# Linear attention on one core: stores deferred behind loads, a part of relu(k) on GpSimd, eps by 32-row matmuls, all queues reordered

## The chip, the cores and the metric

One NeuronCore of a Trainium2 chip. Times are device microseconds of one execution, median of several; the profile's span is about 2 us shorter than the time (177.9 of 179.64 us in the profiled run of the kernel before). Each ratio compares runs of the same rounds; the changed kernel was timed in rounds of its own. Changes under 2% count as "same" unless the interval says otherwise.

## The reference

```python
# q, k, v: bf16 [1, 32, 2048, 128]
def reference(q, k, v):
    phi_q = jnp.where(q > 0, q + 1, jnp.exp(q)) + 1e-6
    phi_k = jnp.where(k > 0, k + 1, jnp.exp(k)) + 1e-6
    kv = jnp.einsum("bhsd,bhse->bhde", phi_k, v)
    z = jnp.einsum("bhsd->bhd", phi_k)
    num = jnp.einsum("bhqd,bhde->bhqe", phi_q, kv)
    den = jnp.einsum("bhqd,bhd->bhq", phi_q, z)[..., None] + 1e-6
    return num / den
```

There are 32 heads. 50.3 MB are read and 16.8 MB written.

## The kernel before

Both phi are computed as min(exp(x), 1) + eps plus relu(x): the two summands stay apart and both go through TensorE. The kernel keeps its tiles in two on-chip memories: SBUF, which loads fill and stores empty, and PSUM, to which TensorE writes its products. v gets a column of ones, so kv also holds z. A head takes, by engine:

- ScalarE: exp(k), exp(q) of the transposed q in PSUM, half or all of relu(q), the copy of kv out of PSUM.
- VectorE: min and relu of k for two heads at a time, min(q), the other half of relu(q), reciprocals and the divide (numerator in PSUM times the reciprocal).
- TensorE: 16 transposes of q, 32 products for kv, 32 half-products (two for each of 16 row tiles, one per summand of phi) for the numerators. These lie in six PSUM banks of two or three tiles; one eps matmul per bank starts the bank and puts 1e-6 in its denominator columns. The numerators come in three groups of two banks (A, B, C).
- GpSimd: the copy of v beside the ones. SyncE: all loads, and all stores but the last part of the last head, in one queue.

The program is a set of named operations with dependencies; the order on each engine is a fixed list.

```python
    NI = 8                                   # input buffers, in heads
    NO = 6                                   # output buffers
    LAG = 2
    VLAG = 3; VAFTER = "rA"                  # the copy of v starts after a reciprocal of group A
    RELU_Q = "SSSA" * (NH // 4)              # S: half on ScalarE, half on VectorE; A: all on ScalarE
    ...
        for h in range(NH + LAG - 1):
            if h + NI < NH:
                loads(h + NI)
            if h >= LAG:
                store(h - LAG)
    ...
        def numerator(e, h, tiles):          # one bank
            s = h % 2
            e.matmul(_ap(o_ps[:, :], SLOT[tiles[0]] + D, [[NC, len(tiles)]]), lhsT=ones[:], rhs=epsr[:, 0:len(tiles)],
                     start=True, stop=False, skip_group_check=True)
            for t in tiles:
                o = o_ps[:, SLOT[t]:SLOT[t] + NC]
                e.matmul(o, lhsT=emq_sb[:, s, t * P:(t + 1) * P], rhs=kvs_sb[:, s, :], start=False, stop=False, ...)
                ins = e.matmul(o, lhsT=rq_sb[:, s, t * P:(t + 1) * P], rhs=kvs_sb[:, s, :], start=False, stop=True, ...)
            return ins
        def num(which, h, banks, deps, bank=None):
            def f(e):
                for b in banks:
                    ins = numerator(e, h, BANKS[b])
                return ins
    ...
        def relu_k(h, n):                    # n = 2 heads in one instruction on VectorE
            ...
            add("DVE", key, lambda e: e.tensor_scalar(
                rk_sb[:, s:s + n], k_sb[:, b:b + n], 0.0, None, op0=ALU.max), ...)
```

Of the kernel before, what the change touches and what calls it, by code (L numbers as in the profile page):

```python
# [7 lines left out]
EPS = 1e-6  # L8
# [7 lines left out]
class Program:  # L16
# [20 lines left out]
    def resolve(self):  # L37
# [5 lines left out]
        for bank, keys in self.banks.items():  # L43
            order = self.schedule[bank]
            assert sorted(order) == sorted(keys), (bank, set(order) ^ set(keys))
            for a, b in zip(order, order[1:]):
                if self.ops[a]["eng"] != self.ops[b]["eng"]:
                    self.ops[b]["deps"].append(a)
        value, count = {}, {}
# [48 lines left out]
def _eps_pieces():  # L98

    import struct  # L100

    def bf(x):
        u = struct.unpack("<I", struct.pack("<f", x))[0]
        u = (u + 0x7FFF + ((u >> 16) & 1)) & 0xFFFF0000
        return struct.unpack("<f", struct.pack("<I", u))[0]

    a = bf(EPS / 128)
    b = bf(EPS - 126 * a)
    return a, b, bf(EPS - 126 * a - b)


def bass_standalone__linear_attn_elu__prompt_kernel(nc: bass.Bass, q: bass.AP, k: bass.AP, v: bass.AP, out: bass.AP):
# [4 lines left out]
    bf16, fp32, i32 = mybir.dt.bfloat16, mybir.dt.float32, mybir.dt.int32  # L117
# [3 lines left out]
    NO = 6  # L121
    L = NH - 1

    LAG = 2
    VLAG = 3
    VAFTER = "rA"
    VFROM = 3
    VTO = 31
    LATE = {L - 1: dict(D="DVE", B="DVE", C="ACT"), L: dict(D="DVE", B="DVE", C="ACT")}
    V1_DVE = 1  # L130
    FUSED = [0] * NH
# [4 lines left out]
    WARM1 = 22  # L136
    FIRST = [("k", 0), ("q", 0), ("v", 0)]
    RELU_Q = "SSSA" * (NH // 4)
# [3 lines left out]
            "warm0 T0 warm1 T1 kx0 kv0 nC0 nA0 T2 nB0 kx1 kv1 nC1 kx2 kv2 nA1 T3 nC2 nB1 kx3 kv3 nB2 nA2 T4 nC3 kx4 kv4 nB3 "  # L142
            "nA3 T5 nC4 kx5 kv5 nB4 nA4 T6 nC5 kx6 kv6 nB5 nA5 T7 nC6 kx7 kv7 nB6 nA6 T8 nC7 kx8 kv8 nB7 nA7 T9 nC8 kx9 kv9 "
            "nB8 nA8 T10 nC9 kx10 kv10 nB9 nA9 T11 nC10 kx11 kv11 nB10 nA10 T12 nC11 kx12 kv12 nB11 nA11 T13 nC12 kx13 kv13 "
            "nB12 nA12 T14 nC13 kx14 kv14 nB13 nA13 T15 nC14 kx15 kv15 nB14 nA14 T16 nC15 kx16 kv16 nB15 nA15 T17 nC16 kx17 "
            "kv17 nB16 nA16 T18 nC17 kx18 kv18 nB17 nA17 T19 nC18 kx19 kv19 nB18 nA18 T20 nC19 kx20 kv20 nB19 nA19 T21 nC20 "
            "kx21 kv21 nB20 nA20 T22 nC21 kx22 kv22 nB21 nA21 T23 nC22 kx23 kv23 nB22 nA22 T24 nC23 kx24 kv24 nB23 nA23 T25 "
            "nC24 kx25 kv25 nB24 nA24 T26 nC25 kx26 kv26 nB25 nA25 T27 nC26 kx27 kv27 nB26 nA26 T28 nC27 kx28 kv28 nB27 nA27 "
            "T29 kx29 kv29 nB28 nA28 T30 nC28 kx30 kv30 nA29 nB29 nC29 T31 kx31 kv31 nD30 nC30 nB30 nD31 nC31 nB31 ").split(),
        DVE=(  # L150
            "eps0 ones v1ones0 v1ones1 eps1 eps2 rk0 em0 emq0 rqb0 rk1 v10 emq1 rqb1 rk2 rC0 fC0 em1 em2 rk3 rqb2 emq2 rA0 "
            "fA0 em3 rC1 fC1 rk5 rC2 fC2 em5 rA1 fA1 emq3 rA2 fA2 rk7 rC3 fC3 rqb4 emq4 rA3 fA3 em7 rC4 emq5 rqb5 fC4 rA4 fA4 "
            "rk9 rC5 rqb6 emq6 fC5 rA5 fA5 em9 rC6 fC6 emq7 rA6 fA6 rk11 rC7 rqb8 emq8 fC7 rA7 fA7 em11 rC8 rqb9 emq9 fC8 rA8 "
            "fA8 rk13 rC9 rqb10 emq10 fC9 rA9 fA9 em13 rC10 emq11 fC10 rA10 fA10 rk15 rC11 rqb12 emq12 fC11 rA11 fA11 em15 "
            "rC12 rqb13 emq13 fC12 rA12 fA12 rqb14 rC13 emq14 fC13 rk17 rA13 fA13 emq15 rC14 fC14 em17 rA14 fA14 rk19 rC15 "
            "rqb16 emq16 fC15 rA15 fA15 em19 rC16 rqb17 emq17 fC16 rA16 fA16 rqb18 rC17 emq18 fC17 rk21 rA17 fA17 emq19 rC18 "
            "fC18 em21 rA18 fA18 rk23 rC19 rqb20 emq20 fC19 rA19 fA19 em23 rC20 rqb21 emq21 fC20 rA20 fA20 rqb22 rC21 emq22 "
            "fC21 rk25 rA21 fA21 emq23 rC22 em25 fC22 rA22 fA22 rk27 rC23 rqb24 emq24 fC23 rA23 fA23 em27 rC24 rqb25 emq25 "
            "fC24 rA24 fA24 emq26 rC25 rqb26 rk29 fC25 rA25 fA25 emq27 rC26 em29 fC26 rA26 fA26 rk31 rC27 rqb28 emq28 rA27 "
            "fA27 em31 rqb29 fC27 rA28 fA28 emq29 rC28 fC28 rqb30 emq30 rC29 fC29 rA29 fA29 emq31.0 emq31.1 rD30 fD30 rC30 "  # L160
            "rB30 fB30 rD31 fD31 rC31 rB31 fB31 ").split(),
        ACT=(
            "ek0.0 ek0 eq0 rqa0 ek1 eq1 kvs0 rqa1 ek2 eq2 kvs1 rqa2 ek3 kvs2 ek4 ek5 eq3 rqa3 kvs3 ek6 eq4 rqa4 kvs4 ek7 eq5 "
            "rqa5 kvs5 ek8 eq6 rqa6 kvs6 ek9 eq7 rqa7 kvs7 ek10 eq8 rqa8 kvs8 ek11 eq9 rqa9 kvs9 ek12 eq10 rqa10 kvs10 ek13 "
            "eq11 rqa11 kvs11 ek14 eq12 rqa12 kvs12 ek15 eq13 rqa13 kvs13 ek16 eq14 rqa14 kvs14 ek17 eq15 rqa15 kvs15 ek18 "
            "eq16 rqa16 kvs16 ek19 eq17 rqa17 kvs17 ek20 eq18 rqa18 kvs18 ek21 eq19 rqa19 kvs19 ek22 eq20 rqa20 kvs20 ek23 "
            "eq21 rqa21 kvs21 ek24 eq22 rqa22 kvs22 ek25 eq23 rqa23 kvs23 ek26 eq24 rqa24 kvs24 ek27 eq25 rqa25 kvs25 ek28 "
            "eq26 rqa26 kvs26 ek29 eq27 rqa27 kvs27 ek30 eq28 rqa28 kvs28 ek31 eq29 rqa29 kvs29 eq30 rqa30 kvs30 eq31.0 "
            "eq31.1 rq31.0 rq31.1 kvs31 fC30.12 fC30.13 fC30.14 fC30 fC31.12 fC31.13 fC31.14 fC31 stC31 ").split(),
        POOL=(  # L170
            "ident0 ident v11 v12 v13 v14 v15 v16 v17 v18 v19 v110 v111 v112 v113 v114 v115 v116 v117 v118 v119 v120 v121 "
            "v122 v123 v124 v125 v126 v127 v128 v129 v130 v131 ").split(),
        kv=(
            "kx0 kv0 kvs0 nC0 rC0 fC0 kx1 kv1 kvs1 nC1 kx2 kv2 kvs2 rC1 fC1 nC2 rC2 fC2 kx3 kv3 kvs3 nC3 kx4 kv4 rC3 fC3 kvs4 "
            "nC4 kx5 kv5 rC4 kvs5 fC4 nC5 kx6 kv6 rC5 kvs6 fC5 nC6 kx7 kv7 rC6 fC6 kvs7 nC7 kx8 kv8 rC7 kvs8 fC7 nC8 kx9 kv9 "
            "rC8 kvs9 fC8 nC9 kx10 kv10 rC9 kvs10 fC9 nC10 kx11 kv11 rC10 kvs11 fC10 nC11 kx12 kv12 rC11 kvs12 fC11 nC12 kx13 "
            "kv13 rC12 kvs13 fC12 nC13 kx14 kv14 rC13 kvs14 fC13 nC14 kx15 kv15 rC14 fC14 kvs15 nC15 kx16 kv16 rC15 kvs16 "
            "fC15 nC16 kx17 kv17 rC16 kvs17 fC16 nC17 kx18 kv18 rC17 kvs18 fC17 nC18 kx19 kv19 rC18 fC18 kvs19 nC19 kx20 kv20 "
            "rC19 kvs20 fC19 nC20 kx21 kv21 rC20 kvs21 fC20 nC21 kx22 kv22 rC21 kvs22 fC21 nC22 kx23 kv23 rC22 kvs23 fC22 "
            "nC23 kx24 kv24 rC23 kvs24 fC23 nC24 kx25 kv25 rC24 kvs25 fC24 nC25 kx26 kv26 rC25 kvs26 fC25 nC26 kx27 kv27 rC26 "  # L180
            "kvs27 fC26 nC27 kx28 kv28 rC27 kvs28 kx29 kv29 kvs29 fC27 nC28 kx30 kv30 rC28 fC28 kvs30 nC29 rC29 fC29 kx31 "
            "kv31 nC30 kvs31 rC30 fC30.12 fC30.13 fC30.14 fC30 nC31 rC31 fC31.12 fC31.13 fC31.14 fC31 ").split())
# [4 lines left out]
    with ExitStack() as es:  # L187
# [38 lines left out]
        add("DVE", "eps0", lambda g: g.memset(epsr[:], ea))  # L226
        add("DVE", "eps1", lambda g: g.memset(epsr[0:1, :], eb), ["eps0"])
        add("DVE", "eps2", lambda g: g.memset(epsr[32:33, :], ec), ["eps0"])
        add("DVE", "ones", lambda g: g.memset(ones[:], 1.0))
        for s in range(2):  # L230
            add("DVE", f"v1ones{s}", lambda g, s=s: g.memset(v1_sb[:, s, :, D:NC + 1], 1.0))


        def load(name, dst, src, h, freed, parts=1):
            n = NT // parts
            for r in range(parts):
# [3 lines left out]
                    [f.format(h - NI) for f in freed if h >= NI] + (GATE if f"{name}{h}" == "k1" else []), dma=f"{name}{h % NI}" if parts == 1 else f"{name}{h}.{r}")  # L240

        def loads(h):
            load("k", k_sb, kf, h, ["ek{}", "rk{}"])
            load("q", q_sb, qf, h, ["T{}"])
            load("v", v_sb, vf, h, ["v1{}"])

        def ld(name, h):
            return [f"ld{name}{h}.0", f"ld{name}{h}.1"] if h == 0 and name == "k" else [f"ld{name}{h}"]
# [5 lines left out]
        for name, h in FIRST:  # L254
            load(name, dict(k=k_sb, q=q_sb, v=v_sb)[name], dict(k=kf, q=qf, v=vf)[name], h, [], 2 if h == 0 and name == "k" else 1)
        for h in range(max(h for _, h in FIRST) + 1, min(NI, NH)):
            loads(h)
        for h in range(NH + LAG - 1):
            if h + NI < NH:
                loads(h + NI)  # L260
            if h >= LAG:
                store(h - LAG)
# [7 lines left out]

        def relu_q(h):
# [3 lines left out]
        def numerator(e, h, tiles):  # L275
            s = h % 2
            e.matmul(_ap(o_ps[:, :], SLOT[tiles[0]] + D, [[NC, len(tiles)]]), lhsT=ones[:], rhs=epsr[:, 0:len(tiles)],  # L277
                     start=True, stop=False, skip_group_check=True)
            for t in tiles:
# [10 lines left out]
        def num(which, h, banks, deps, bank=None):  # L290
            def f(e):
                for b in banks:
                    ins = numerator(e, h, BANKS[b])
                return ins
# [203 lines left out]
```

## Time and profile before

| | before |
|---|---|
| time, first three runs | 180.02 us (179.67 to 180.59) |
| ScalarE, one head of kind S / kind A, start to start | 4.65 / 5.5 us |
| VectorE, one head | 4.79 us |
| TensorE, one head | 4.72 us |
| DMA, one head at the 416 GB/s of the middle | 5.0 us |

The table of stretches gives the busy time of each engine in a stretch, with the number of instructions; then the clock granted to TensorE, the busy share of DMA, and GB/s. Of the kernel before:

```profile
core 0: us, PE busy (x) PEld busy (x) DVE busy (x) ACT busy (x) POOL busy (x), PEclk, DMA share, GB/s
...
40.00:60.00 20.00, 19.93 (x360) 19.49 (x357) 19.61 (x29) 20.00 (x17) 4.16 (x4) 1.00 1.03 413
...
120.00:140.00 20.00, 19.88 (x358) 19.32 (x356) 19.60 (x30) 20.00 (x19) 4.17 (x4) 1.00 1.03 415
```

ScalarE (ACT) has no idle time there. TensorE (PE) and VectorE (DVE) look almost as busy, but a matmul's busy time overlaps the next one's, so for TensorE the starts have to be read. The chain that ended last agrees; these are the shares by engine of the page of the kernel before:

```profile
ACT 48%; PE 20%; DVE 16%; DMA 12%; issue 1%; SPq 0%; DVEq 0%
```

The timeline of ScalarE of the kernel before shows one head: start, duration, line. L399 is relu(q), L373 the copy of kv, L347 exp(k), L394 exp(q).

```profile
99.70 1.05 ACT L399 ACTIVATE la<-la 128x1024 bf16<-128x1024 bf16 x1
100.61 0.32 ACT L373 ACTIVATE la<-la 128x129 bf16<-128x129 f32 x1
100.77 1.96 ACT L347 ACTIVATE la<-la 128x2048 bf16<-128x2048 bf16 x1
102.56 1.93 ACT L394 ACTIVATE la<-la 128x2048 bf16<-128x2048 bf16 x1
104.32 1.08 ACT L399 ACTIVATE la<-la 128x1024 bf16<-128x1024 bf16 x1
```

From 99.70 to 104.32 us is one head of kind S: 4.62 us, near the table's 4.65. The timeline of TensorE of the kernel before, around one eps matmul (L277; L281 and L283 are the half-products):

```profile
100.11 0.22 PE L283 MATMUL la<-la 128*128 128x129 bf16 x1
100.16 0.17 PE L277 MATMUL la<-la 128*128 128x3 bf16 x1
100.19 0.22 PE L281 MATMUL la<-la 128*128 128x129 bf16 x1
100.25 0.22 PE L283 MATMUL la<-la 128*128 128x129 bf16 x1
```

A half-product takes 0.056 us of TensorE's time, the eps matmul 0.03, although each record is 0.17 to 0.22 us long. Over 40 to 140 us the means are 0.060 us from a half-product to the eps matmul and 0.03 from that to the next.

### The profile page before, as it was taken

The page shows a single profiled execution, that of the slowest core. Times are in us where ns is not written, and L with a number is a line of the kernel's source. Part 1 is how long each engine was busy: PE and PEld are TensorE (multiplying, and loading weights), DVE is VectorE, ACT ScalarE, POOL GpSimd, SP SyncE. Part 2 cuts the span into 40 slices and gives each one's busy share as a digit, 9 for nine tenths or more (in the row PEclk, how much of TensorE's full clock was granted, in tenths as well). Part 3 has the DMA queues.
Part 4 walks back from the last instruction along what each step waited for, and adds up shares of the span by engine and source line. Part 5 has one row for each costly group of instructions (what it writes and reads, how often), then busy time and mean ns, then how long its engine had stood idle before and what let it go on. Part 6 is the DMA issues. An engine that isn't in the chain of part 4 may idle for free.

```text
span 177.9 us, 6326 instructions
## 1 busy us (share of the span) xinstructions
PE 163.9 (92%) x2822; PEld 157.7 (89%) x2822; DVE 155.8 (88%) x230; ACT 161.2 (91%) x140; POOL 33.1 (19%) x37
## 2 busy tenths in 40 slices
PE   6849987999999999999999999999999899999981
PEld 6848886999999999999998999989999799999971
DVE  1255699799999999999999999999999899999983
ACT  5396999989999999999999999999999989996572
POOL 1022022222121222222121122222222022222000
PEclk9996999999999999999999999999999999999998
DMA  5999999999999999999999999999999999984336
GB/s 156 366 417 412 410 407 411 406 410 404 414 415 416 416 413 416 418 412 421 414 411 420 415 418 416 415 419 415 415 416 415 420 413 420 411 333 179 125 122 236
DMA packets 18891, 67.52 MB, mean 380 GB/s; under 512 B 2096, under 2 KB 2480, under 8 KB 18864
## 3 DMA queue, kind: packets, MB, share of 16 engines
q1 hardware_dynamic: 18720, 66.99, 93.7%
q8 instruction: 22, 0.36, 0.8%
q10 hardware_dynamic: 144, 0.13, 0.2%
q14 instruction: 5, 0.04, 0.1%
HBM read 50.33 MB, written 16.78 MB: 377 GB/s over the span
## 4 chain that ended last, share of the span: by engine, by line
ACT 48%; PE 20%; DVE 16%; DMA 12%; issue 1%; SPq 0%; DVEq 0%
ACT la L347 19%; ACT la L394 18%; PE la L362 9%; DMA out_dram<-la 9%; ACT la L399 8%; DVE la L307 8%; PE la L281 4%; PE la L283 3%; PE la L354 3%; DMA la<-in_q_dram 3%; ACT la L373 2%; DVE la L339 2%; DVE la L402 2%; DVE la L406 2%; DVE la L303 1%
## 5 line engine op out<-in xcount | busy, mean ns | idle before, releaser
L307 DVE TENSOR_TENSOR la<-la 128x512 bf16<-128x512 f32 (+2 forms) x64 | 77.2, 1206 | 3.7 <-DMA out_dram<-la 1.2
L283 PE MATMUL la<-la 128*128 128x129 bf16 x512 | 68.0, 220 | 0.0
L281 PE MATMUL la<-la 128*128 128x129 bf16 x512 | 68.0, 219 | 0.0
L362 PE MATMUL la<-la 128*128 128x129 bf16 x1024 | 65.5, 222 | 0.6 <-DVE la L307 0.5
L394 ACT ACTIVATE la<-la 128x2048 bf16<-128x2048 bf16 x31 | 58.8, 1895 | 5.1 <-PE la L354 3.0
L347 ACT ACTIVATE la<-la 128x2048 bf16<-128x2048 bf16 (+1 forms) x33 | 61.7, 1877 | 1.4 <-DMA la<-in_k_dram 1.4
L362 PEld LDWEIGHTS la<-la 128*128 128x128 bf16 x1024 | 61.3, 99 | 1.2 <-DVE la L307 0.8
L378 POOL COPY la<-la 128x1024 int32<-128x1024 int32 x31 | 32.4, 1046 | 128.7 <-DVE la L303 115.1
L283 PEld LDWEIGHTS la<-la 128*128 128x128 bf16 x512 | 49.5, 97 | 0.0
L281 PEld LDWEIGHTS la<-la 128*128 128x128 bf16 x512 | 47.1, 97 | 0.0
L399 ACT ACTIVATE la<-la 128x1024 bf16<-128x1024 bf16 (+1 forms) x31 | 38.5, 1241 | 0.0
L277 PE MATMUL la<-la 128*128 128x3 bf16 (+1 forms) x192 | 32.5, 169 | 5.1 <-DVE la L307 3.0
L354 PE MATMUL la<-la 128*128 128x128 bf16 x512 | 33.9, 219 | 3.0 <-DVE la L402 2.1
L354 PEld LDWEIGHTS la<-la 128*128 128x128 bf16 x512 | 29.6, 98 | 4.4 <-DVE la L402 3.2
L277 PEld LDWEIGHTS la<-la 128*128 128x128 bf16 x192 | 18.7, 97 | 9.1 <-DVE la L307 7.1
L406 DVE TENSOR_SCALAR la<-la 128x2048 bf16<-128x2048 bf16 x31 | 21.1, 682 | 5.8 <-ACT la L394 5.8
L339 DVE TENSOR_SCALAR la<-la 128x4096 bf16<-128x4096 bf16 (+1 forms) x18 | 19.8, 1100 | 3.0 <-DMA la<-in_k_dram 3.0
L331 DVE TENSOR_SCALAR la<-la 128x4096 bf16<-128x4096 bf16 (+1 forms) x18 | 19.8, 1098 | 1.0 <-ACT la L347 0.9
L402 DVE TENSOR_SCALAR la<-la 128x1024 bf16<-128x1024 bf16 x24 | 16.1, 673 | 2.1 <-ACT la L394 2.1
L303 DVE RECIPROCAL la<-la 128x4 f32<-128x4 f32 (+2 forms) x66 | 13.1, 200 | 2.9 <-PE la L283 2.6
L373 ACT ACTIVATE la<-la 128x129 bf16<-128x129 f32 x32 | 9.6, 301 | 3.1 <-PE la L362 1.6
L437 PE MATMUL la<-la 128*128 128x120 bf16 x70 | 6.2, 273 | 1.5 <-POOL la L222 1.5
(18 smaller groups left out, 16.1 us busy)
## 6 DMA issues: line engine op xcount, KB each, us to landing
la<-in_q_dram SPq DMA_DIRECT2D x32, 512.0 KB, 15.4
la<-in_v_dram SPq DMA_DIRECT2D x32, 512.0 KB, 15.8
la<-in_k_dram SPq DMA_DIRECT2D x31, 512.0 KB, 15.3
out_dram<-la SPq DMA_DIRECT2D x31, 512.0 KB, 15.2
la<-in_k_dram SPq DMA_DIRECT2D x2, 256.0 KB, 2.9
out_dram<-la SPq DMA_DIRECT2D x2, 192.0 KB, 2.1
out_dram<-la ACTq DMA_DIRECT2D x1, 128.0 KB, 1.9
```

The lines of the kernel that those rows point to most:

```text
L277: e.matmul(_ap(o_ps[:, :], SLOT[tiles[0]] + D, [[NC, len(tiles)]]), lhsT=ones[:], rhs=epsr[:, 0:len(tiles)], start=True, stop=False, skip_ ...
L281: e.matmul(o, lhsT=emq_sb[:, s, t * P:(t + 1) * P], rhs=kvs_sb[:, s, :], start=False, stop=False, skip_group_check=True)
L283: ins = e.matmul(o, lhsT=rq_sb[:, s, t * P:(t + 1) * P], rhs=kvs_sb[:, s, :], start=False, stop=True, skip_group_check=True)
L307: add("DVE", f"f{which}{h}", lambda e: e.tensor_tensor(out=_ap(o_sb[:, :, :, :], ob + t0 * D, [[n * D, nb], [D, n], [1, D]]), in0=_ap(o_ps ...
L339: add("DVE", key, lambda e: e.tensor_scalar(rk_sb[:, s:s + n], k_sb[:, b:b + n], 0.0, None, op0=ALU.max), [d for i in range(n) for d in ld ...
L347: add("ACT", "ek0.0" if h == 0 and r == 0 else f"ek{h}", lambda e, c=c: e.activation(em_sb[:, h % 4, c], k_sb[:, h % NI, c], ACT.Exp), ([f ...
L354: ins = e.transpose(xT[:, j * P:(j + 1) * P], q_sb[:, h % NI, j * D:(j + 1) * D], ident[:])
L362: ins = e.matmul(kv_ps, lhsT=src[:, h % 4, j * D:(j + 1) * D], rhs=v1_sb[:, h % 2, j, 0:NC], start=(j + part == 0), stop=(j == NT - 1 and ...
L378: add("DVE" if h < V1_DVE else "POOL", f"v1{h}", lambda e, h=h, s=s: e.tensor_copy(v1_sb[:, s, :, 0:D].bitcast(i32), v_sb[:, h % NI].rearr ...
L394: add("ACT", f"eq{h}", lambda e, s=s: e.activation(emq_sb[:, s], xT[:, :], ACT.Exp), [f"T{h}"] + nums(h - 2))
L399: add("ACT", key, lambda e, s=s, c=c: e.activation(rq_sb[:, s, c], xT[:, c], ACT.Relu), [f"T{h}"] + nums(h - 2))
L406: add("DVE", f"emq{h}", lambda e, s=s: e.tensor_scalar(emq_sb[:, s], emq_sb[:, s], 1.0, EPS, op0=ALU.min, op1=ALU.add), [f"eq{h}"])
```

## The change

Its intent: take work from ScalarE (relu(q) is split in every head), pay for it on VectorE by giving a quarter of relu(k) (4 of 16 tiles, for 28 heads) to GpSimd, keep DMA from holding faster engines back (stores drop behind the loads by up to 12 heads), make the eps matmuls cheaper by using only 32 rows, and start sooner (head 0's q in halves, more warm-up matmuls). All queues are in a new order, and the copies of v and the new GpSimd pieces are released by chosen VectorE operations.

```diff
-    NO = 6
+    NO = 12
-    LAG = 2
+    LAG = [2+h//3 for h in range(40)]
-    WARM1 = 22
+    WARM1 = 40
+    WARM2 = 8
+    HALF = "kq"
+    RKP = [()]*4+[((12,16),)]*(NH-4)
-    RELU_Q = "SSSA" * (NH // 4)
+    RELU_Q = "S" * 32
...          # new lists for all engines, and a list "after": "... v14<emq2 rkp5<emq3 rkp6<em5 v15<em5 ..."
+        done = 0
+        for h in range(NH - NI):
+            loads(h + NI)
+            while done <= h - LAG[h]:
+                store(done)
+                done += 1
+        for h in range(done, L):
+            store(h)
...
-        def numerator(e, h, tiles):
+        def numerator(e, h, banks):
             s = h % 2
-            e.matmul(_ap(o_ps[:, :], SLOT[tiles[0]] + D, [[NC, len(tiles)]]), lhsT=ones[:], rhs=epsr[:, 0:len(tiles)],
-                     start=True, stop=False, skip_group_check=True)
-            for t in tiles:
+            for b in banks:
+                r, n = slice(32 * (b % 4), 32 * (b % 4) + 32), len(BANKS[b])
+                e.matmul(_ap(o_ps[:, :], SLOT[BANKS[b][0]] + D, [[NC, n]]), lhsT=ones[r, :], rhs=epsr[r, 0:n],
+                         start=True, stop=False, skip_group_check=True)
+            for t in [t for b in banks for t in BANKS[b]]:
...
+        def relu_pool(e, out, x, form):
+            if form == 0:
+                return e.tensor_scalar(out.bitcast(i16), x.bitcast(i16), 0, None, op0=ALU.max)
+            if form == 1:
+                return e.tensor_scalar(out, x, 1.0, 0.0, op0=ALU.mult, op1=ALU.max)
+            return e.tensor_scalar(out, x, 0.0, 1.0, op0=ALU.max, op1=ALU.mult)
...                                          # in relu_k, for each head of a pair (form is h // 2 % 3):
+                    add("POOL", f"rkp{h + i}", lambda e: relu_pool(
+                        e, rk_sb[:, s + i, t0 * D:t1 * D], k_sb[:, b + i, t0 * D:t1 * D], h // 2 % 3), ...)
             add("DVE", key, lambda e: e.tensor_scalar(
-                rk_sb[:, s:s + n], k_sb[:, b:b + n], 0.0, None, op0=ALU.max), ...
+                rk_sb[:, s:s + n, c], k_sb[:, b:b + n, c], 0.0, None, op0=ALU.max), ...    # c: the first 12 tiles
```

The maximum with 0 as int16 is relu for bf16, since a set sign bit makes the int16 negative.

## The prediction

> What bounds the kernel now. In the table of stretches ScalarE is busy 20.00 of 20 us from 40 to 80 and 120 to 140 us, and 19.88 between. The timeline gives its head, start to start: exp(k) 1.80 us, exp(q) 1.77, half relu(q) 0.91, copy of kv 0.17: 4.65; every fourth head does the whole relu(q), 1.77. The mean period is about 4.95 us. Three others stand close behind. VectorE: divide 1.68 + 0.61, reciprocals 0.34, min(q) 0.59, relu(k) and min(k) 0.57 each, half relu(q) 0.58 in three of four heads: 4.79. TensorE: 64 matmuls near 57 ns, 16 transposes 0.89, six eps matmuls of about 35 ns: 4.72. DMA moves 410 to 420 GB/s in the slices until 150 us; a head's 2.1 MB take 5.0 us of it. Loads run 8 heads ahead, so ScalarE hardly waits for them (1.4 us in the waits), but a faster engine would soon meet DMA. Outside the steady part some 17 us of ScalarE are idle.
>
> What changes. (1) ScalarE loses eight half relus, 7 us: 4.65 per head throughout. (2) VectorE gains them, 4.6 us, and loses a quarter of relu(k) over 28 heads (0.27 us per pair, 3.7 us): it stays at 4.80 and becomes the tightest engine. (3) GpSimd, busy 19%, gets 28 pieces of 512 elements; its copy of 1024 words takes 1.04 us, so I estimate 0.5 to 0.8 us a piece. They are hidden unless they meet VectorE's SBUF-to-SBUF operations: the Trainium skill, SBUF — State Buffer, Who interferes with whom, says the two then block each other for a whole instruction. The trace before avoids it: each copy starts with the 1.68 us divide, which reads PSUM. Most new pieces are released just ahead of that divide, but piece plus copy nearly fill it, and some are released ahead of relu(q): I allow 2 to 4 us in total. (4) While loads last, a head needs 1.57 MB and about 0.35 of stores, 4.6 us at 416 GB/s, so DMA no longer holds the engines to 5.0. The 67 MB remain: DMA cannot end before about 165 us. (5) 32-row eps matmuls gain at most 0.2 us per head; TensorEngine Tiling (Array Packing), Key Properties, says that a change of tiling mode drains TensorE, six changes a head. Nothing in this trace shows it; if each costs over 0.05 us, TensorE becomes the bound. (6) Head 0 in halves and more warm-up matmuls: exp(q) started after 2.67 us idle, the first kv product took 3.49 us where later ones take 1.84; together 2.5 us.
>
> Sum. VectorE in place of ScalarE as the bound: 0.15 x 30 = 4.5 us; start 2.5; no waits for stores and tighter end about 3; contention back 3. I predict 173.5 us, range 168.5 to 178.5. Chances: faster by over 2% 0.70, within 2% 0.26, slower 0.04.
>
> Signs. Right: ScalarE's idle grows in the middle; VectorE over 97% busy from 20 to 160 us; DMA below 415 GB/s in the middle and high to the end. Contention: a relu(q) or min(k) of VectorE longer than 0.68 or 1.22 us, or GpSimd pieces far over 0.8. Drains: more than 60 ns from an eps matmul to its successor.
>
> What would make it wrong: drains that make TensorE 5 us per head (then 178 or more); an output buffer not yet stored around head 25, as stores queue some 15 us behind loads; or a schedule so much tighter that it runs at DMA's floor, 167.

## The result, and the profile after

The changed kernel took 186.21 us (185.85 to 186.63, 4 runs) against 180.22 of the kernel before in the same rounds: a ratio of 1.0336, 95% interval 1.030 to 1.037. It is slower. (Ratios in this document are the mean time of one kernel's runs over that of the other's of the same rounds, so not quite the ratio of the medians.)

The table of stretches of the changed kernel:

```profile
core 0: us, PE busy (x) PEld busy (x) DVE busy (x) ACT busy (x) POOL busy (x), PEclk, DMA share, GB/s
...
40.00:60.00 20.00, 19.34 (x318) 17.72 (x315) 19.25 (x27) 18.87 (x17) 10.98 (x8) 1.00 1.03 414
...
120.00:140.00 20.00, 20.00 (x335) 18.67 (x334) 19.13 (x27) 18.81 (x16) 9.26 (x8) 1.00 1.03 414
140.00:160.00 20.00, 20.00 (x336) 18.66 (x334) 18.40 (x27) 18.36 (x17) 12.77 (x9) 1.00 0.96 390
```

From 120 us on TensorE is the one without idle time, with fewer matmuls in 20 us (335 against 358), and ScalarE has more than a microsecond to spare. Its chain by engine, and ScalarE's waits (who waited for whom: us in total, times, longest), say the same:

```profile
PE 71%; DVE 12%; ACT 8%; DMA 5%; issue 2%; SPq 0%; DVEq 0%
```

```profile
ACT la L448 <- PE la L408: 14.2, 22, 2.2
```

exp(q) (L448) waited 22 times for the transposes (L408), 14.2 us in all. In the kernel before, waits of exp(q) for TensorE were 5.0 us. Why TensorE does less in its time is in its timeline. L308 is the eps matmul (x2: the two of a group), L312 and L314 the half-products:

```profile
103.12 0.22 PE L312 MATMUL la<-la 128*128 128x129 bf16 x1
103.17 0.22 PE L314 MATMUL la<-la 128*128 128x129 bf16 x1
103.33 0.18 PE L308 MATMUL la<-la 32*128 32x2 bf16 x2
103.44 0.23 PE L312 MATMUL la<-la 128*128 128x129 bf16 x1
103.50 0.22 PE L314 MATMUL la<-la 128*128 128x129 bf16 x1
```

The eps matmuls start 0.15 us after the half-product ahead of them, and the next half-product 0.11 us after their start. Over 40 to 140 us the means are 0.154 and 0.110. A group so costs 0.154 + 0.110 - 0.056 = 0.21 us more than no eps at all, where the two eps matmuls of a group had cost about 0.07. Three groups a head add 3 x 0.14 = 0.42 us: TensorE's head goes from 4.72 to about 5.14 us by this sum. The copies of kv of heads 23 and 27 begin at 134.76 and 155.56 us, 5.20 us per head.

Before a matmul, TensorE loads its weights (PEld in the profile). These are the loads of the two eps matmuls shown, first of the kernel before, then of the changed one:

```profile
100.11 0.10 PEld L277 LDWEIGHTS la<-la 128*128 128x128 bf16 x1
```

```profile
103.32 0.09 PEld L308 LDWEIGHTS la<-la 32*128 32x128 bf16 x2
```

Before, the load starts together with the half-product ahead (100.11) and 0.05 us before its own matmul (100.16). With 32 rows it starts 0.15 us after that half-product (103.17) and only 0.01 before its own matmul (103.33). So the wait comes before the weight load already: at the change of form the load no longer runs ahead.

GpSimd's groups of the changed kernel, one row per shape (x count, busy us, mean ns of one):

```profile
L431 POOL COPY la<-la 128x1024 int32<-128x1024 int32 x31 | 32.4, 1044 | 46.9 <-DMA la<-in_v_dram 17.0 <-DVE la L364 14.9 <-DVE la L395 9.4
L374 POOL TENSOR_SCALAR la<-la 128x512 bf16<-128x512 bf16 x10 | 19.2, 1925 | 11.1 <-DVE la L461 4.0 <-DVE la L332 3.7 <-DVE la L364 2.4
L373 POOL TENSOR_SCALAR la<-la 128x512 bf16<-128x512 bf16 x8 | 15.4, 1925 | 13.0 <-DVE la L461 6.5 <-DVE la L364 3.0 <-DVE la L395 2.3
L371 POOL TENSOR_SCALAR la<-la 128x512 int16<-128x512 int16 x10 | 14.9, 1488 | 15.7 <-DVE la L461 12.5 <-DVE la L332 2.1 <-DVE la L364 1.2
```

The pieces take 1.49 us (int16, one operation) and 1.93 us (bf16, two operations), not the estimated 0.5 to 0.8. They meet VectorE. From the two timelines of the changed kernel, GpSimd first:

```profile
39.66 1.93 POOL L373 TENSOR_SCALAR la<-la 128x512 bf16<-128x512 bf16 x1 [3.04 <-DVE la L364]
41.54 1.04 POOL L431 COPY la<-la 128x1024 int32<-128x1024 int32 x1
```

```profile
40.20 1.75 DVE L335 TENSOR_TENSOR la<-la 128x1536 bf16<-128x1536 f32 x1
41.86 1.26 DVE L461 TENSOR_SCALAR la<-la 128x2048 bf16<-128x2048 bf16 x1
...
47.72 0.66 DVE L461 TENSOR_SCALAR la<-la 128x2048 bf16<-128x2048 bf16 x1
```

The divide (L335) reads PSUM and keeps its length beside GpSimd. min(q) (L461), SBUF to SBUF, starts while the copy runs and takes 1.26 us instead of 0.66. So a meeting shows as a longer instruction of VectorE, not as idle time. The copy ends at 42.58 us and min(q) 0.54 later, at 43.12. In the changed kernel's trace every min(q) that a copy of v or a piece stretched ends 0.54 or 0.55 us after GpSimd's instruction, every such relu(k) 0.81 or 0.82 and every such paired min(k) 1.08, as if VectorE did its whole work only once GpSimd is done. Half relu(q) reads PSUM, and none ran longer than 0.69 us, although many ran beside GpSimd. I call stretch the sum, over VectorE's SBUF-to-SBUF instructions of a trace, of what each took beyond the median of its shape, where that is over 0.06 us. It is 0 before and 2.5 us in the changed kernel.

### The profile page after: what moved, and what is told of

It is laid out like the page before. It is cut to its first block, busy times and chain, and to the rows that moved or that the text cites. A ratio compares the mean times of both kernels' runs of the same rounds, so it can differ in the third digit from the quotient of the medians.

```text
span 184.4 us, 6446 instructions
## 1 busy us (share of the span) xinstructions
PE 175.8 (95%) x2848; PEld 162.2 (88%) x2848; DVE 162.0 (88%) x251; ACT 156.6 (85%) x139; POOL 81.8 (44%) x65
## 4 chain that ended last, share of the span: by engine, by line
PE 71%; DVE 12%; ACT 8%; DMA 5%; issue 2%; SPq 0%; DVEq 0%
PE la L418 24%; PE la L312 17%; PE la L314 13%; PE la L408 12%; DVE la L335 6%; ACT la L448 5%; PE la L308 5%; DMA la<-in_q_dram 4%; ACT la L402 2%; DVE la L461 2%; DMA la<-in_k_dram 1%; DVE la L456 1%; DVE la L364 1%; ACT la L453 1%; DVE la L332 1%
## 5 line engine op out<-in xcount | busy, mean ns | idle before, releaser
L335 DVE TENSOR_TENSOR la<-la 128x512 bf16<-128x512 f32 (+2 forms) x64 | 77.0, 1203 | 2.0
L448 ACT ACTIVATE la<-la 128x2048 bf16<-128x2048 bf16 (+1 forms) x32 | 58.2, 1823 | 14.8 <-PE la L408 14.2
L312 PE MATMUL la<-la 128*128 128x129 bf16 x512 | 69.5, 223 | 0.0
L314 PE MATMUL la<-la 128*128 128x129 bf16 x512 | 68.5, 221 | 0.0
L402 ACT ACTIVATE la<-la 128x2048 bf16<-128x2048 bf16 (+1 forms) x33 | 61.2, 1859 | 1.8 <-DMA la<-in_k_dram 1.8
L418 PEld LDWEIGHTS la<-la 128*128 128x128 bf16 x1024 | 59.9, 97 | 1.6 <-ACT la L425 0.6
L314 PEld LDWEIGHTS la<-la 128*128 128x128 bf16 x512 | 50.2, 98 | 0.0
L312 PEld LDWEIGHTS la<-la 128*128 128x128 bf16 x512 | 47.7, 97 | 1.5
L408 PE MATMUL la<-la 128*128 128x128 bf16 x512 | 34.0, 219 | 0.9 <-DMA la<-in_q_dram 0.7
L453 ACT ACTIVATE la<-la 128x1024 bf16<-128x1024 bf16 x31 | 31.6, 1020 | 0.0
L408 PEld LDWEIGHTS la<-la 128*128 128x128 bf16 x512 | 29.9, 98 | 1.6 <-DVE la L431 0.9
L461 DVE TENSOR_SCALAR la<-la 128x2048 bf16<-128x2048 bf16 (+1 forms) x32 | 22.1, 689 | 4.9 <-ACT la L448 4.9
L374 POOL TENSOR_SCALAR la<-la 128x512 bf16<-128x512 bf16 x10 | 19.2, 1925 | 11.1 <-DVE la L461 4.0
L456 DVE TENSOR_SCALAR la<-la 128x1024 bf16<-128x1024 bf16 x31 | 20.9, 676 | 1.8 <-ACT la L448 1.7
L371 POOL TENSOR_SCALAR la<-la 128x512 int16<-128x512 int16 x10 | 14.9, 1488 | 15.7 <-DVE la L461 12.5
L373 POOL TENSOR_SCALAR la<-la 128x512 bf16<-128x512 bf16 x8 | 15.4, 1925 | 13.0 <-DVE la L461 6.5
L308 PEld LDWEIGHTS la<-la 32*128 32x128 bf16 x192 | 9.0, 90 | 11.8 <-DVE la L461 1.1
L308 PE MATMUL la<-la 32*128 32x3 bf16 (+1 forms) x192 | 17.0, 173 | 1.3 <-DVE la L335 0.7
L364 DVE TENSOR_SCALAR la<-la 128x4096 bf16<-128x4096 bf16 x14 | 17.5, 1253 | 0.1
```

Of the source, the lines that this page charges most:

```text
L308: e.matmul(_ap(o_ps[:, :], SLOT[BANKS[b][0]] + D, [[NC, n]]), lhsT=ones[r, :], rhs=epsr[r, 0:n], start=True, stop=False, skip_group_check= ...
L335: add("DVE", f"f{which}{h}", lambda e: e.tensor_tensor(out=_ap(o_sb[:, :, :, :], ob + t0 * D, [[n * D, nb], [D, n], [1, D]]), in0=_ap(o_ps ...
L402: add("ACT", key, lambda e, c=c: e.activation(em_sb[:, h % 4, c], k_sb[:, h % NI, c], ACT.Exp), l + o + [prev("kv", h, 4)])
L408: ins = e.transpose(xT[:, j * P:(j + 1) * P], q_sb[:, h % NI, j * D:(j + 1) * D], ident[:])
L418: ins = e.matmul(kv_ps, lhsT=src[:, h % 4, j * D:(j + 1) * D], rhs=v1_sb[:, h % 2, j, 0:NC], start=(j + part == 0), stop=(j == NT - 1 and ...
L448: add("ACT", key, lambda e, s=s, c=c: e.activation(emq_sb[:, s, c], xT[:, c], ACT.Exp), [f"T{h}{r}"] + o + nums(h - 2))
```

## The experiments

Three theories for the loss. A: each entry into and exit from the 32-row form costs TensorE time, and TensorE has become the bound. B: GpSimd's long pieces hold VectorE up. C: the new order of the queues is worse. The first four runs shared their rounds (before: 180.34 us).

### r1_full_eps: the change with 128-row eps matmuls

```diff
-    a = bf(EPS / 32)                    # b, c likewise: the same total over 128 rows
+    a = bf(EPS / 128)
-                e.matmul(..., lhsT=ones[r, :], rhs=epsr[r, 0:n],
+                e.matmul(..., lhsT=ones[:], rhs=epsr[:, 0:n],
```

> The changed kernel with its eps matmuls over all 128 rows again (values of eps divided over 128 rows), everything else kept, also their order. Theory A (each of three groups per head enters and leaves a 32-row form and TensorE loses 0.16 us per group, 0.48 per head, and is the bound): 172 to 176 us, TensorE 4.74 per head, VectorE becomes the bound. Theory B (GpSimd's pieces of 1.5 to 1.9 us hold up VectorE): stays at 184 to 187. Theory C (the new order of the engines' work): stays at 184 to 187.

Measured: 179.50 us, ratio 0.9974 (0.9905 to 1.0043). The form of the eps matmuls alone is worth 6.7 us; without it the change is even with the kernel before. From a half-product to the eps matmuls it is now 0.071 us in the mean and from those to the next 0.055. Theory A holds; but 172 to 176 was missed, so something else is left. The table of stretches tells where to look: VectorE is now the engine with hardly any idle time (TensorE looks as busy, but its busy time overlaps).

```profile
120.00:140.00 20.00, 19.68 (x355) 19.17 (x353) 19.70 (x30) 19.43 (x18) 9.68 (x7) 1.00 1.02 414
140.00:160.00 20.00, 19.86 (x364) 19.56 (x361) 19.86 (x29) 17.91 (x17) 12.53 (x10) 1.00 0.99 400
```

Its stretch is 5.2 us here, twice that of the changed kernel. That the faster pace with the same releases is the reason is argued, not tested.

### r2_no_pieces: the change without GpSimd's pieces

```diff
-    RKP = [()]*4+[((12,16),)]*(NH-4)
+    RKP = [()]*NH                       # and rkp... out of GpSimd's list and of "after"
```

> The changed kernel with all of relu(k) on VectorE again, the 32-row eps matmuls kept. Theory A: TensorE still takes 5.20 us per head, so 184 to 187 us although VectorE has nothing to meet. Theory B: 174 to 178. Theory C: 184 to 187.

Measured: 185.70 us, ratio 1.0306. The pieces are not what made the change slow; behind TensorE they hardly matter. Theory B falls as the main cause.

### r3_before_eps32: the kernel before with 32-row eps matmuls alone

```diff
-    a = bf(EPS / 128)
+    a = bf(EPS / 32)                    # b, c likewise, in all four strips of 32 rows
-        def numerator(e, h, tiles):
+        def numerator(e, h, banks):     # eps of both banks with lhsT=ones[r, :], rhs=epsr[r, 0:n], then all tiles
```

> The kernel before with only the eps matmuls in the 32-row form, two of a group side by side. Theory A: TensorE takes 4.72 + 0.48 = 5.20 us per head against ScalarE's 4.95, so about 8 us slower than before: 185 to 190. Theories B and C: 179 to 181, as before.

Measured: 187.38 us, ratio 1.0403 (1.0338 to 1.0468). This one edit, in the old order, with the old stores and no pieces, gives a loss of the size of the whole change's. The table of stretches of this run shows the switch of bound: ScalarE's 20.00 of before has become 19.06, and TensorE has no idle time.

```profile
100.00:120.00 20.00, 20.00 (x336) 18.67 (x334) 18.68 (x27) 19.06 (x16) 4.16 (x4) 1.00 1.02 416
120.00:140.00 20.00, 20.00 (x335) 18.67 (x333) 18.76 (x26) 19.06 (x17) 4.16 (x4) 1.00 1.03 417
```

The gaps are those of the changed kernel: 0.151 and 0.109 us. Theory C falls as the main cause.

### r4_full_eps_no_pieces: both undone

> The changed kernel with 128-row eps matmuls and all of relu(k) on VectorE: order, stores and the start are left of the change. Theory A: 172 to 177; beside the run with the pieces it tells what the pieces are worth once TensorE is out of the way (VectorE gains 0.13 us per head by them, 3.7 us, less what it waits for GpSimd). Theory B: 173 to 177. Theory C: 184 to 187.

Measured: 177.96 us, ratio 0.9871 (0.9807 to 0.9935). Against r2_no_pieces, also without pieces, the form of the eps matmuls is worth 7.7 us. And the time is 1.5 us less than that of r1_full_eps: the pieces, meant as a relief, cost 1.5 us. The stretch is 0.3 us. The account: VectorE saves 14 x 0.27 = 3.8 us by the pieces and is stretched 5.2 - 0.3 = 4.9 us more by them, a net loss of 1.1. VectorE is close to idle-free here:

```profile
100.00:120.00 20.00, 19.62 (x354) 19.11 (x352) 19.82 (x29) 18.66 (x16) 4.16 (x4) 1.00 1.03 416
120.00:140.00 20.00, 19.59 (x357) 19.24 (x355) 19.83 (x31) 19.45 (x18) 4.16 (x4) 1.00 1.03 415
```

That it is the bound, the next run confirms.

The next four shared their rounds (before: 179.84 us).

### r5_spare_pieces: the meeting without the relief

```diff
+        spare_sb = sb([P, 4, 4 * D])
-                        e, rk_sb[:, s + i, t0 * D:t1 * D], k_sb[...], h // 2 % 3),
+                        e, spare_sb[:, s + i], k_sb[...], h // 2 % 3),
-            c = slice(0, min([a for a, _ in RKP[h]] + [NT]) * D)
+            c = slice(0, N)             # VectorE does all tiles; 128-row eps matmuls as in r1
```

> 128-row eps matmuls; GpSimd runs its 28 pieces as in the changed kernel, but writes them to spare tiles that nothing reads, and VectorE does all of relu(k). It has the meeting of the two engines without the relief. In the run with pieces VectorE's SBUF-to-SBUF instructions were 5.2 us longer in sum than their usual lengths, against 0.3 without pieces. If that is what the pieces cost, and VectorE is the bound, this takes 178.0 + 5 = 182 to 184 us, and its stretch is again 4 to 6 us. If the pieces hurt in another way (a late piece that the kv product waits for), VectorE's instructions keep their lengths, and it takes 177 to 180.

Measured: 182.27 us, ratio 1.0135 (1.0116 to 1.0154), stretch 5.2 us. Against r4_full_eps_no_pieces (other rounds) that is 4.3 us by medians, and by ratios 2.7%, 4.8 us, where the stretch grew by 4.9. No engine waits for a piece in this trace, so the rival in the expectation, a late piece, falls. The pieces do nothing but run, and VectorE loses about what its stretch says.

### r6_old_stores: 128-row eps, no pieces, stores as before

```diff
-    LAG = [2+h//3 for h in range(40)]
+    LAG = [2] * 40
-    NO = 12
+    NO = 6
```

> 128-row eps matmuls, no pieces, and the stores again two heads behind the loads with 6 output buffers. If DMA's 5.0 us per head would hold VectorE (4.94 per head) as I predicted: 179 to 182 us, with VectorE waiting for stores by 1 us or more in sum. If deferring the stores is worth nothing while the engines take 5.0 us per head: within 0.7 us of the 178.0 of the run with deferred stores.

Measured: 180.79 us, ratio 1.0048 (1.0024 to 1.0072), where the deferred stores had 0.9871 in the rounds before. Deferring, with the 12 output buffers that it needs, is worth 2.8 us by medians in the new order (3.2 by ratios, since the rounds differ). VectorE waits 1.5 us for output buffers here and ScalarE 4.3 us for k, in ten waits, against 1.3 in one wait with the stores deferred (r4_full_eps_no_pieces), which waits for no output buffer. With the old stores, then, what is left of the change (order, split of relu(q), start) is 0.5% slower than the kernel before, though its fourth copy of kv begins 2.5 us sooner (28.98 us against 31.49). So theory C is not the main cause, but the new order brings no gain of its own here.

### r7_32row_each_bank: twice as many entries and exits

```diff
             for b in banks:
                 ...                     # the bank's 32-row eps matmul
-            for t in [t for b in banks for t in BANKS[b]]:
-                ...
+                for t in BANKS[b]:
+                    ...                 # and its half-products, before the next bank's eps
```

> The changed kernel with its 32-row eps matmuls each just ahead of their bank's products, so TensorE enters and leaves the 32-row form six times per head, not three. If the loss is paid per entry and exit: 0.16 to 0.19 us each, about 0.43 more per head, 13 us more: 196 to 202 us. If the loss is paid per eps matmul, or for another reason: 184 to 188.

Measured: 203.63 us, ratio 1.1326: 17.4 us over the changed kernel. The timeline of TensorE of this run shows the same two gaps around a single eps matmul:

```profile
127.91 0.22 PE L314 MATMUL la<-la 128*128 128x129 bf16 x1
128.06 0.17 PE L308 MATMUL la<-la 32*128 32x2 bf16 x1
128.17 0.23 PE L312 MATMUL la<-la 128*128 128x129 bf16 x1
```

The means are 0.153 and 0.107 us. One eps matmul costs a bank 0.20 us, as two had cost a group: the number of eps matmuls stayed the same, the number of entries doubled, and so did the loss. Three more entries a head are 3 x 0.20 x 32 = 19.6 us; I had expected 13, from a guess that a pair shared less of the cost.

### r8_balance: six heads with all of relu(q) on ScalarE

```diff
-    RELU_Q = "S" * 32
+    RELU_Q = "".join("A" if h in (4, 9, 14, 19, 24, 29) else "S" for h in range(NH))
```

> 128-row eps matmuls, no pieces, and in six heads (4, 9, 14, 19, 24, 29) the whole relu(q) on ScalarE. VectorE loses 6 x 0.58 = 3.5 us and ScalarE gains 6 x 0.87 = 5.2. If VectorE is the bound at 178.0: 174.5 to 176.5. If the order of TensorE's work or DMA is the bound there: 177 to 179.

Measured: 181.35 us, ratio 1.0101 (1.0058 to 1.0143), above both expected ranges, by 4.9 us and 2.4. Against r4_full_eps_no_pieces, VectorE's busy time fell from 161.1 to 159.0 us, but its idle gaps over 0.12 us grew from 8.8 to 13.7 us in sum; among its new waits are 2.5 us for ScalarE's copies of kv. The lists were made for heads that are all alike. That a longer ScalarE head in a fixed order is the reason is argued, not tested.

The last four shared their rounds, on another chip (before: 179.53 us).

### r9_no_pieces_again: r4 once more

> The version with 128-row eps matmuls and no pieces once more, unchanged, in the same rounds as the three below: 177.5 to 178.5 us, ratio to before 0.983 to 0.991.

Measured: 178.09 us, ratio 0.9916 (0.9896 to 0.9936). The median is as expected; the kernel before was faster in these rounds, so the ratio just misses.

### r10_before_deferred: the kernel before with deferred stores alone

```diff
-    NO = 6
+    NO = 12
-    LAG = 2
+    LAG = [2+h//3 for h in range(40)]   # and the loop of the change
```

> The kernel before with only the stores deferred and 12 output buffers. It waits 1.2 us for output buffers in its trace, and otherwise ScalarE is the bound at 4.96 us per head. If deferring is worth only those waits there: 178.5 to 180. If it is worth as much as in the new order (about 3 us): 176.5 to 178.

Measured: 178.61 us, ratio 0.9945 (0.992 to 0.997). Deferring is worth 0.9 us where ScalarE is the bound, which is near the 1.2 us that VectorE had waited for output buffers.

### r11_int16: pieces in the int16 form only

```diff
-                        e, rk_sb[...], k_sb[...], h // 2 % 3),
+                        e, rk_sb[...], k_sb[...], 0),      # 128-row eps matmuls as in r1
```

> 128-row eps matmuls, pieces of four tiles on GpSimd, all 28 in the int16 form (1.49 us against 1.93 for the two others). VectorE's stretch should fall below the 5.2 us of the three forms, to 2 to 4; relief stays 3.8. So 177 to 179 us; if the form does not matter, 179.5 as with the three forms.

Measured: 176.19 us, ratio 0.9814 (0.9788 to 0.9841), lower than expected; whether it is faster than before by the full 2% stays unclear, since the interval spans 0.98. It beats both kernels and r9_no_pieces_again by 1.9 us. GpSimd's group of this run:

```profile
L371 POOL TENSOR_SCALAR la<-la 128x512 int16<-128x512 int16 x28 | 41.6, 1486 | 37.4 <-DVE la L461 19.8 <-DVE la L332 6.6 <-DVE la L364 6.5
```

The stretch is 2.5 us, 2.7 less than with three forms, and the time 3.3 us less by medians, 1.6% by ratios (other rounds, another chip). The shorter form turns the pieces from a loss into a gain: relief 3.8 us, and 1.6 more stretch than the 0.9 of r9_no_pieces_again, so 2.2 us net against the measured 1.9. The stretch of one trace is itself uncertain by about half a microsecond: r4 and r9 are the same kernel with 0.3 and 0.9, most of it one min(k) near the start. Whether the int16 data type or the single operation makes the form shorter is not separated.

### r12_int16_two_tiles: pieces of half the size

```diff
-    RKP = [()]*4+[((12,16),)]*(NH-4)
+    RKP = [()]*4+[((14,16),)]*(NH-4)    # int16 form, 128-row eps matmuls
```

> The same with pieces of two tiles: I estimate 0.8 to 0.9 us a piece (half of 1.49 and a fixed part), relief 14 x 0.133 = 1.9 us, stretch 0.5 to 2 us. 176.5 to 178.5 us: at best 1 us below the version without pieces.

Measured: 177.23 us, ratio 0.9861 (0.9838 to 0.9885), stretch 0.1 us. The pieces now meet hardly anything, but relieve half as much. GpSimd's group of this run:

```profile
L371 POOL TENSOR_SCALAR la<-la 128x256 int16<-128x256 int16 x28 | 23.7, 845 | 46.2 <-DVE la L461 23.6 <-DVE la L332 9.5 <-DVE la L364 8.6
```

## Why the prediction was wrong

I predicted 173.5 us (168.5 to 178.5), faster; it was 186.2, slower by 3.4%. The reading of before was right: ScalarE bounds it with three others within 0.25 us per head. The failing step is (5), and with it the line "VectorE in place of ScalarE as the bound" of the sum. Of the 12.7 us between prediction and result, (5) accounts for 6.7 and the undersized contention of (3), once TensorE is out of the way, for about 2; the rest is not assigned.

- (5) eps. The text named the risk and its threshold ("if each costs over 0.05 us, TensorE becomes the bound") and then put nothing for it in the sum, since nothing in the trace before showed it. The runs: 0.21 us per entry and exit together, that is about 0.10 per change of form, twice the threshold. TensorE takes 5.2 us per head, not 4.72. This alone is 6.7 us (r1_full_eps; 7.7 without pieces and 7.0 in the old order), and three more entries a head cost 17.4 us more (r7_32row_each_bank). The Trainium skill, TensorEngine Tiling (Array Packing), Key Properties, states that a change of tiling mode drains TensorE; the gaps of 0.15 and 0.11 us, with the weight load held back too, agree with a drain, that is, with the next form waiting until the matmuls ahead have left the array. Whether the load waits for such a drain, or cannot run ahead for another reason, no run here tells apart. A cost of six changes per head on an engine 0.25 us from the bound should have been in the sum: at 0.05 it would already have been 0.3 us a head, more than the at most 0.2 that the smaller matmuls were to gain.
- (3) pieces. The term was mis-sized. I scaled from the copy of 32-bit words and got 0.5 to 0.8 us; they take 1.49 and 1.93. I allowed 3 us of contention. In the changed kernel, where TensorE set a slower pace, it was 2.5, within the allowance by luck; with TensorE out of the way it is 5.2, more than the 3.8 us of relief. The mechanism was right: the Trainium skill, SBUF — State Buffer, Who interferes with whom, says that GpSimd and a VectorE instruction in a two-port mode, which tensor_scalar can enter, block each other for whole instructions. The trace agrees: stretched instructions end a fixed time after GpSimd's, min(q) takes 1.26 us beside a copy, the PSUM-reading divide is unchanged, and the loss of r5_spare_pieces is the stretch within a microsecond. Two details were off: the relu(q) that the text feared for reads PSUM and was never stretched, and most of the stretched instructions in the changed kernel (6 of 9) met a copy of v, not a piece; without pieces (r4, r9) only two a trace met one.
- (2) VectorE as the tightest engine at 4.80: that holds only where TensorE does not bound (r1, r4, r5), and there the stretch took the advantage. Without pieces VectorE needs 4.79 + 0.145 = 4.94 us per head (the last quarter of its half relu(q)), no less than ScalarE's 4.95 before. So the expected 4.5 us of steady gain hung on the pieces being nearly free, which they were not.
- (4) stores. The direction was right, 2.8 us in the new order with 128-row eps (r6_old_stores) against the 3 of the sum, which also held a tighter end. The sign was wrong: DMA stayed at 405 to 422 GB/s in the middle (probably since loads run ahead as far as buffers allow), and near the end it fell to 60 to 117 GB/s, lower than the 122 to 179 before. No wait for an output buffer around head 25 came.
- (6) start. The fourth copy of kv begins at 29.45 us in place of 31.49: 2.0 us of the predicted 2.5.
- The sign "over 60 ns from an eps matmul to its successor" came (0.11 us). ScalarE's idle grew, as said, but waiting for TensorE. VectorE was busy 131.6 of 140 us from 20 to 160, 94%, not over 97%.

What stays open: the part of the miss that (3) and (5) leave; why the new order with only 128-row eps and no pieces (5.00 us per head from head 3 to 27) does not reach VectorE's 4.94, and how much an order made for the true costs would give.

## What to carry to other kernels

When an engine is within a few per cent of the bound, a risk on it belongs in the sum with a size, not in the list of what could go wrong. A tiny matmul in another tiling form is not tiny: count entries and exits of the form, here 0.2 us a pair, before counting rows; the full-height form of the same matmul cost 0.035 us. Work moved to GpSimd has to be timed in its own data type and instruction form (1.49 or 1.93 us here for the same 512 elements), and should fit beside VectorE instructions that read PSUM, such as the divide of 1.75 us here; what it takes back shows as VectorE instructions longer than the median of their shape.

## What the Trainium skill lacked or had wrong

- TensorEngine Tiling (Array Packing), Key Properties: gives no size for the change of mode. Here 32-row matmuls between 128-row ones cost 0.15 us ahead and 0.11 us behind, 0.2 us per entry and exit, the same for one or two of them.
- GPSIMD Engine Reference, Engine selection: says that one-input elementwise work is roughly line-rate. Here 512 bf16 elements with two scalar operations take 1.93 us (3.8 ns an element), 512 as int16 with one operation 1.49, 256 so 0.85 (2.5 ns for each further element), while a copy of 1024 int32 words takes 1.04 (1.0 ns an element), and VectorE's min(k) of 4096 bf16 elements takes 1.22. The page gives no costs by data type for such instructions.
- SBUF — State Buffer, Who interferes with whom: agrees. It does not say how it looks in a profile: VectorE's instruction is recorded longer (1.26 us in place of 0.66) and ends a fixed time after GpSimd's (0.54 us for 2048 elements, 1.08 for 4096), and no wait is shown.
